# The first block of 384 tokens cut into two of 192, in a fused attention and two-layer expert kernel

## The chip, the cores and the metric

The kernel runs on one core of one Trainium2 chip. A core has TensorE (PE, matrix products; PEld is its loading of weights), VectorE (DVE), ScalarE (ACT), GpSimd (POOL) and SyncE (SP, which issues most of the transfers here). They run side by side and wait for one another by semaphores. The metric is the time of one execution on the device, in microseconds (us); lower is better.

## The reference

Inputs are float32. The batch is 8, with 8 heads, 576 positions and 64 numbers a head. Keys and values are pooled over 8 positions, so each sequence has 72 pooled positions.

```python
# attention
k_p = k.reshape(B, H, Sp, 8, D).mean(axis=3)
v_p = v.reshape(B, H, Sp, 8, D).mean(axis=3)
scores = scale * np.matmul(q, k_p.transpose(0, 1, 3, 2))
scores = scores - np.max(scores, axis=-1, keepdims=True)
attn = np.exp(scores)
attn = attn / (np.sum(attn, axis=-1, keepdims=True) + 1e-09)
x = np.matmul(attn, v_p)            # then (B*S, H*D) = (4608, 512)
# part 1: 512 -> 768 -> 512
h = np.maximum(np.maximum(x @ w1, x @ w2), x @ w3)
x = h @ w_out
# part 2: 512 -> 2048 -> 512
h = np.maximum(x @ w_in, 0.0)
out = h * h @ w_out2
```

## The kernel before

**Numbers.** A float32 operand is split into a high part and a remainder (`split`, lines 121 and 122: ScalarE copies the high part, another engine subtracts), and a product is three matmuls: high by high, high by low, low by high. The weights arrive as 64-bit numbers. Each row of 512 of them (a tile `wraw`) is loaded by SP and turned into float32 by two ScalarE and two VectorE instructions (`convert`, lines 148 to 153), and then split by ScalarE and POOL (lines 121 and 122). Part 1 has 24 such rows: 18 for w1, w2 and w3, and 6 for its output matrix.

**Part 1.** The 4608 tokens go in 12 blocks of 384. For a block, `attention(j)` fills four tiles x, one for each pair of heads, with 128 numbers by 384 tokens. For a pair it loads q (and, at the start of a sequence, k and v, which VectorE reduces over 8 positions: lines 221 and 228), splits q, multiplies q by the pooled keys in tiles of 128 or 96 tokens (line 344), takes the maximum (346), exponentials with their sums (349), adds a constant and takes the reciprocal (353, 354), scales on POOL (355), transposes (370), copies and splits the transposed scores (372, 373), and multiplies by the values (385, or 395 and 396).

A sequence has 576 tokens, so a block's tokens are one or two pieces: a piece of 384 is cut into three tiles of 128, a piece of 192 into two of 96. Block 0 is the first 384 tokens of sequence 0. Block 1 is that sequence's last 192 tokens and the first 192 of sequence 1.

In blocks with a number under `LIGHT` = 2, one softmax covers all the tiles of a pair in a piece, and POOL splits q. In the others a softmax covers one tile, and VectorE splits q.

`moe1(j)` then runs 22 steps for a block (`STEPS`). Each of the first 18 is one of three matrices by one of six groups of 128 columns: 12 matmuls (line 465), all four x, one weight row, and 384 columns. The results are copied by ScalarE (471) or joined by a maximum on VectorE (473); after three of them h is split. The last four steps multiply h by the output matrix, 18 matmuls each (484); ScalarE copies the result to ys and issues its store to y_dram. Results wait in three PSUM buffers (`mm_ps`).

**Order.** Each piece of work goes with a due time onto the list `todo`, counted in steps, and `run` writes them in the order of these times. The attention of block j+1 is spread over block j's 22 steps, shifted to the front by 10 steps; its loads stand 10 steps ahead of it and the preparation of q, k and v four. The weight rows of part 1 have due times from -12, 0.9 steps apart. The weights of part 2 are prepared in the background from block `SECOND[0]` to the last one. A scheduler then orders each engine's instructions by these priorities and by when it expects operands to be ready. Each engine works off its own list in order.

**Part 2** takes the tokens in 9 blocks of 512. It reads them back from y_dram (`load_y`, line 549 on), in as many pieces as the blocks of part 1 that they touch. Its first block is loaded and prepared during the last block of part 1.

Of the kernel before, what the change touches and what calls it, by code (L numbers as in the profile page):

```python
# [10 lines left out]
F32 = mybir.dt.float32  # L11
F32R = mybir.dt.float32r
# [8 lines left out]
P = 128  # L21
B, H, S, D = 8, 8, 576, 64
# [3 lines left out]
NT = B * S  # L26
DM = H * D
KD = DM // P
# [3 lines left out]
KF2 = FF2 // P  # L32
NE = 3
T1 = 384
NB1 = NT // T1
T2 = 512
NB2 = NT // T2

# [22 lines left out]

LEAD_SECOND = 5

SECOND = (2, NB1 - 1)

NATURAL = 1

# [17 lines left out]
def attention_moe_kernel(ctx: ExitStack, tc: tile.TileContext, q, k, v, vn, w1, w2, w3, wo1, wi2, wo2, out):  # L85
# [3 lines left out]
    dram = ctx.enter_context(tc.tile_pool(name="dram", bufs=1, space=DRAM))  # L89
    mm_ps = ctx.enter_context(tc.tile_pool(name="mm_ps", bufs=3, space=PSUM))  # L90
# [12 lines left out]

    wi2_dram = [[dram.tile([P, 2, n], F32, name=f"wi2_dram{f}_{i}") for i, n in enumerate(WIDTHS)] for f in range(KF2 // 2)]
    wo2_dram = [dram.tile([P, 2, 512], F32, name=f"wo2_dram{f}") for f in range(KF2)]
    y_dram = [dram.tile([KD, P, T1], F32, name=f"y_dram{j}") for j in range(NB1)]

# [14 lines left out]
    def split(hl, src, engine=nc.vector):  # L124

        split_to(hl[:, 0], hl[:, 1], src, engine)
# [43 lines left out]
    h_p = s1.enter_context(tc.tile_pool(name="h_p", bufs=KF1))  # L170
    t_p = s1.enter_context(tc.tile_pool(name="t_p", bufs=2))
# [87 lines left out]
    def pieces(j):  # L259

        t = 0
        while t < T1:
            b, s0 = divmod(j * T1 + t, S)
            n = min(T1 - t, S - s0)
            yield b, s0, n, t
            t += n

# [4 lines left out]
    def attention(j):  # L272

        x_t[j] = [None] * NPAIR
        n_tiles = sum(NPAIR * len(score_tiles(n)) for _, _, n, _ in pieces(j))
        pace = (STEPS - 1) / n_tiles
        at = (j - 1) * STEPS + pace / 2 - (LAG_T + LAG_V + LEAD_X)
        for b, s0, n, t in pieces(j):
            if s0 == 0 and b < NATURAL:
                tiles = []  # L280
                when = at - pace / 2 + LAG_T + LAG_V if t else at + pace / 2
                todo.append((when - LEAD_LOAD, lambda b=b, tiles=tiles: tiles.extend(load_natural(b))))
                todo.append((when, lambda tiles=tiles: pool_v(tiles)))
            for p in range(NPAIR):
                load, prepare, softmax, transpose, values = attend(j, b, s0, n, p, t)
                todo.append((at - LEAD_LOAD, load))
                todo.append((at - LEAD_PREP, prepare))
                tiles = score_tiles(n)
                if j < LIGHT:
                    todo.append((at, functools.partial(softmax, tiles)))  # L290
                for c, m in tiles:
                    if j >= LIGHT:
                        todo.append((at, functools.partial(softmax, [(c, m)])))
                    todo.append((at + LAG_T, functools.partial(transpose, c, m)))
                    at += pace
                todo.append((at - pace + LAG_T + LAG_V, values))
# [107 lines left out]
    w1_t, wo1_t = {}, {}  # L404
# [48 lines left out]
    def moe1(j):  # L453

        x = x_t.pop(j)
        hs = []
        for f in range(KF1):
            hm = t_p.tile([P, T1], F32, tag="hm", name="hm")
            h = h_p.tile([P, 2, T1], F32R, tag="h", name="h")
            for e in range(NE):  # L460
                ps = mm_ps.tile([P, T1], F32, tag="ps", name="ps")
                n = 0
                for kk in range(KD):
                    for a, c in PARTS:
                        nc.tensor.matmul(  # L465
                            ps, lhsT=w1_t[f, e][:, a, kk * P : (kk + 1) * P], rhs=x[kk][:, c],
                            start=(n == 0), stop=(n == 3 * KD - 1),
                        )
                        n += 1
                if e == 0:  # L470
                    nc.scalar.activation(hm, ps, AF.Copy)
                else:
                    nc.vector.tensor_tensor(out=hm, in0=ps, in1=hm, op=ALU.max)  # L473
                if e == NE - 1:
                    split(h, hm)
                yield
            hs.append(h)
            now[0] = hm
        for d in range(KD):
            ps = mm_ps.tile([P, T1], F32, tag="ps", name="ps")  # L480
            n = 0
            for kk in range(KF1):
                for a, c in PARTS:
                    nc.tensor.matmul(  # L484
                        ps, lhsT=wo1_t[kk][:, a, d * P : (d + 1) * P], rhs=hs[kk][:, c],
                        start=(n == 0), stop=(n == 3 * KF1 - 1),
                    )
                    n += 1
            ys = t_p.tile([P, T1], F32, tag="ys", name="ys")
            nc.scalar.activation(ys, ps, AF.Copy)  # L490
            nc.scalar.dma_start(out=y_dram[j][d], in_=ys)
            yield

    def run():
        for _, f in sorted(todo, key=lambda a: a[0]):
            f()
        todo.clear()

    def add_moe1(j):
        steps = moe1(j)  # L500
        todo.extend((j * STEPS + i, functools.partial(next, steps, None)) for i in range(STEPS))
# [6 lines left out]
    for kk in range(KF1):  # L508
        todo.append((0.9 * (NE * KF1 + kk) - 12, functools.partial(load_wo1, kk)))
    for j in range(NB1 - 1):  # L510
        add_moe1(j)
# [11 lines left out]
    for i, (src, raw, prepare) in enumerate(second):  # L523
        when = STEPS * (SECOND[0] + (i + 0.5) * (SECOND[1] - SECOND[0]) / len(second))
        todo.append((when - LEAD_SECOND, functools.partial(load_second, src, raw)))
# [23 lines left out]
    def load_y(j, r):  # L549

        yr = y_p.tile([P, 2, T2], F32, tag=f"yr{r}", name=f"yr{r}")
        for i in range(2):
            t = 0
            while t < T2:
                b, o = divmod(j * T2 + t, T1)
                n = min(T2 - t, T1 - o)
                nc.sync.dma_start(out=yr[:, i, t : t + n], in_=y_dram[b][2 * r + i, :, o : o + n])
                t += n
        yr_t[j, r] = yr
# [16 lines left out]

    ORDER = (1, 6, 7, 5, 2, 4, 3)
    early = [functools.partial(load_y, 0, r) for r in range(2)] + [functools.partial(mix_y, 0)]
    early.append(functools.partial(fetch_in, 0, w2_p))
    early += [functools.partial(split_y, 0, m) for m in ORDER]  # L580
    for i, f in enumerate(early):
        todo.append(((NB1 - 1) * STEPS + (i + 0.5) * (NE * KF1) / len(early), f))
    add_moe1(NB1 - 1)
    run()
# [85 lines left out]
    for j in range(NB2):  # L670
        for gr in range(NG):
            if gr == 0 and j + 1 < NB2:
                for r in range(2):
                    load_y(j + 1, r)
            g = moe2_in(j, gr)
            if gr == NG - 2 and j + 1 < NB2:
                mix_y(j + 1)
            if gr == NG - 1 and j + 1 < NB2:
                for m in ORDER:
                    split_y(j + 1, m)  # L680
            for h, half in ((1, 1), (0, 0), (1, 0), (0, 1)):
                moe2_out(j, gr, h, half, g[h, half])
            nxt = j * NG + gr + 1
            if nxt < NB2 * NG:
                fetch_group(*divmod(nxt, NG))
# [41 lines left out]
```

## Time and profile before

| | |
|---|---|
| median of 3 runs | 1547.24 us (1545.96 to 1547.61) |
| profiled execution | 1545.93 us, its span 1544.2 us |
| PE | 1509.4 us busy, 98% of the span, 9290 matmuls |
| DVE | 947.7 us, 61% |
| ACT | 623.0 us, 40% |
| POOL | 200.2 us, 13% |
| mean granted clock of TensorE | 0.985 |

The span runs from the first to the last instruction of the program; some 1.7 us lie around it. Busy time is the union of an engine's instructions. Matmuls are pipelined: one of 384 columns is recorded with 334 ns from start to end though the next one starts 174 ns later, so the price of a matmul is read from the distance of starts, or from the busy time of a dense run divided by its count. The granted clock is the share of TensorE's full speed that the chip allowed: 1.00 is 2.4 GHz and 0.50 is 1.2 GHz.

### The profile page before, as it was taken

Reading aid. Unit: us, or ns where it says so; the run is one execution under the profiler, and the core shown is the slowest. Engines: PE = TensorE matmul, PEld = TensorE weight load, DVE = VectorE, ACT = ScalarE, POOL = GpSimd, SP = SyncE. Lnnn points to the kernel's source line nnn. Section 1 sums busy time; section 2 is a strip of 40 time slices with the busy share of each in tenths; the row PEclk is TensorE's granted clock in tenths of the full one; section 3 lists DMA queues with packets and bytes.
Section 4 is the critical chain, followed back from the end, with each engine's and each line's share of the span. In section 5 each row is a group of like instructions: output and inputs, shape, how many; then the busy total and the mean of one; then the engine's idle time right before and its main releaser. Section 6 shows DMA issues by size and latency. Waiting matters only on the chain.

```text
span 1544.2 us, 25098 instructions
## 1 busy us (share of the span) xinstructions
PE 1509.4 (98%) x9290; PEld 1416.2 (92%) x9290; DVE 947.7 (61%) x1991; ACT 623.0 (40%) x1772; POOL 200.2 (13%) x303
## 2 busy tenths in 40 slices
PE   6899999999999999999999999999999999999998
PEld 4789999999999999999999898988989888999987
DVE  6895578776786766755427455455655546464544
ACT  7775566656566566654212212121212112121211
POOL 5550122222222121312000000000000000000000
PEclk7799999999999999999999999999999999999999
DMA  7552234434334333323475434333333433343321
GB/s 227 163 169 67 76 105 151 142 96 145 122 119 144 99 129 103 104 79 116 135 290 208 150 113 161 110 127 121 108 137 125 149 123 108 111 150 110 137 110 69
DMA packets 80858, 200.87 MB, mean 130 GB/s; under 512 B 9024, under 2 KB 32576, under 8 KB 80736
## 3 DMA queue, kind: packets, MB, share of 16 engines
q1 hardware_dynamic: 73824, 189.83, 36.2%
q10 hardware_dynamic: 6912, 9.44, 1.7%
q8 instruction: 74, 1.21, 0.3%
q14 instruction: 48, 0.39, 0.1%
HBM read 157.29 MB, written 41.94 MB: 129 GB/s over the span
## 4 chain that ended last, share of the span: by engine, by line
PE 88%; DVE 4%; DMA 3%; ACT 2%; issue 1%; SPq 0%; POOL 0%; DVEq 0%; ACTq 0%; POOLq 0%
PE ps L465 26%; PE acc L645 25%; PE ps L600 21%; PE ps L484 9%; PE sc L344 2%; PE tr L370 2%; DMA out_dram<-o 2%; PE av L396 1%; PE av L395 1%; ACT ss L349 1%; DVE wbits L153 0%; DMA kq<-in_q_dram 0%; ACT wraw L149 0%; DVE hm L473 0%; DVE wbits L150 0%
## 5 line engine op out<-in xcount | busy, mean ns | idle before, releaser
L465 PE MATMUL ps<-x,w 128*128 128x384 f32 x2592 | 508.6, 344 | 1.7 <-ACT x L121 0.8
L465 PEld LDWEIGHTS ps<-x,w 128*128 128x128 f32 x2592 | 452.0, 191 | 4.1 <-ACT x L121 1.4
L645 PE MATMUL acc<-wo2s,g 128*128 128x512 f32 x1728 | 412.6, 391 | 0.0
L600 PEld LDWEIGHTS ps<-y,wi2s 128*128 128x128 f32 x3024 | 370.4, 188 | 13.1 <-PE ps L600 4.0
L600 PE MATMUL ps<-y,wi2s 128*128 128x256 f32 x3024 | 376.8, 280 | 3.4 <-DVE s L629 2.9
L645 PEld LDWEIGHTS acc<-wo2s,g 128*128 128x128 f32 x1728 | 316.4, 188 | 62.5
L121 ACT ACTIVATE g<-c 128x512 fp32r<-128x512 f32 x144 | 90.8, 631 | 410.9 <-DVE c L611 403.9
L617 DVE TENSOR_TENSOR s<-ps,s 128x512 f32<-128x512 f32 x72 | 49.8, 691 | 262.4 <-PE ps L600 261.8
L484 PE MATMUL ps<-h,wo 128*128 128x384 f32 x864 | 164.9, 339 | 0.7 <-DVE hm L473 0.5
L484 PEld LDWEIGHTS ps<-h,wo 128*128 128x128 f32 x864 | 148.9, 188 | 1.4 <-DVE hm L473 0.8
L617 DVE TENSOR_TENSOR c<-ps,s 128x512 f32<-128x512 f32 x144 | 98.8, 686 | 24.9 <-PE ps L600 21.7
L355 POOL TENSOR_TENSOR ss<-ss,st 128x144 f32<-128x144 f32 (+3 forms) x144 | 73.2, 510 | 309.4 <-DVE st L354 237.8
L349 ACT ACTIVATE ss<-sc,st 128x72 f32<-128x72 f32 (+1 forms) x320 | 98.0, 313 | 35.0 <-DVE st L346 31.3
L473 DVE TENSOR_TENSOR hm<-ps,hm 128x384 f32<-128x384 f32 x144 | 79.4, 552 | 53.1 <-PE ps L465 49.3
L122 DVE TENSOR_TENSOR g<-c,g 128x512 fp32r<-128x512 f32 x144 | 98.6, 685 | 17.4 <-ACT g L121 16.5
L611 DVE SCALAR_TENSOR_TENSOR c<-c 128x512 f32<-128x512 f32 x144 | 98.8, 687 | 2.1
L373 DVE TENSOR_TENSOR pt<-tr,pt 72x256 fp32r<-72x256 f32 (+1 forms) x160 | 61.5, 386 | 53.4 <-ACT pt L372 52.1
L344 PEld LDWEIGHTS sc<-kbd,qs 128*128 128x128 f32 (+1 forms) x480 | 73.6, 192 | 11.4 <-issue 5.2
L344 PE MATMUL sc<-kbd,qs 128*128 128x144 f32 (+1 forms) x480 | 74.7, 271 | 8.0 <-ACT kbd L195 5.2
L372 ACT ACTIVATE pt<-tr 72x256 fp32r<-72x256 f32 (+1 forms) x160 | 56.2, 354 | 58.1 <-PE tr L370 56.5
L370 PE MATMUL tr<-ident,ss 128*72 128x128 f32 (+1 forms) x320 | 59.9, 274 | 14.4 <-DVE pt L373 10.1
L349 ACT ACTIVATION_READ_ACCUMULATOR ss<-sc,st 128x1 f32 (+1 forms) x320 | 63.1, 197 | 0.0
(78 smaller groups left out, 1249.3 us busy)
## 6 DMA issues: line engine op xcount, KB each, us to landing
wo2s<-wo_dram SPq DMA_DIRECT2D x144, 512.0 KB
wi2s<-wi_dram SPq DMA_DIRECT2D x24, 512.0 KB
wraw<-in_wo_dram SPq DMA_DIRECT2D x22, 512.0 KB
wraw<-in_w_dram SPq DMA_DIRECT2D x18, 512.0 KB
y_dram<-ys ACTq DMA_DIRECT2D x48, 192.0 KB
out_dram<-o SPq DMA_DIRECT2D x36, 256.0 KB
wraw<-in_wi_dram SPq DMA_DIRECT2D x16, 512.0 KB
wi_dram<-wraw SPq DMA_DIRECT2D x16, 512.0 KB
```

Of the source, the lines that this page charges most:

```text
L121: nc.scalar.activation(hi, src, AF.Copy)
L122: engine.tensor_tensor(out=lo, in0=src, in1=as_f32(hi), op=ALU.subtract)
L344: nc.tensor.matmul(src[:, i], lhsT=lhsT, rhs=kbd[:, p, l], start=(n == 0), stop=(n == 2))
L349: nc.scalar.activation(ss[:, i, h], src[:, i, h], AF.Exp, bias=st[:, 0, i, h : h + 1], accum_out=st[:, 1, i, h : h + 1],)
L370: nc.tensor.transpose(tr[:, h, :m], sms[c][:, h], ident[:m, :m])
L465: nc.tensor.matmul(ps, lhsT=w1_t[f, e][:, a, kk * P : (kk + 1) * P], rhs=x[kk][:, c], start=(n == 0), stop=(n == 3 * KD - 1),)
L473: nc.vector.tensor_tensor(out=hm, in0=ps, in1=hm, op=ALU.max)
L484: nc.tensor.matmul(ps, lhsT=wo1_t[kk][:, a, d * P : (d + 1) * P], rhs=hs[kk][:, c], start=(n == 0), stop=(n == 3 * KF1 - 1),)
L600: nc.tensor.matmul(bank[:, u * HT : (u + 1) * HT], lhsT=wi2_t[2 * gr + u][i][:, a, o + kk * P : o + (kk + 1) * P], rhs=y_t[j][m][:, c, kk] ...
L611: nc.vector.scalar_tensor_tensor(out=c, in0=c, scalar=0.0, in1=c, op0=ALU.max, op1=ALU.mult)
L617: nc.vector.tensor_tensor(out=c, in0=bank, in1=other, op=ALU.add)
L645: nc.tensor.matmul(acc_t[j][2 * half + i], lhsT=g[:, a, u * HT + i * P : u * HT + (i + 1) * P], rhs=wo2_t[j, 4 * gr + 2 * u + h][:, c], st ...
```

## The change

Part 1 gets a list of block sizes, `SIZES`: 192, 192, and then 384 eleven times. `NB1` becomes 13, and `BEGIN` holds the first token of each block. The tiles keep their size of 384 and the two short blocks use the first 192 columns. `STEPS` and the due times are counted in blocks as before, so each short block has 22 steps and 288 matmuls of its own. `LIGHT` remains 2, which is now the two short blocks. `SECOND` starts at block 3, which begins at the same token as block 2 did. Blocks 2 to 12 hold the tokens of the old blocks 1 to 11.

```diff
 T1 = 384
-NB1 = NT // T1
+SIZES = [T1 // 2] * 2 + [T1] * (NT // T1 - 1)
+NB1 = len(SIZES)
+BEGIN = [sum(SIZES[:j]) for j in range(NB1)]
...
-SECOND = (2, NB1 - 1)
+SECOND = (3, NB1 - 1)
...
-    y_dram = [dram.tile([KD, P, T1], F32, name=f"y_dram{j}") for j in range(NB1)]
+    y_dram = [dram.tile([KD, P, n], F32, name=f"y_dram{j}") for j, n in enumerate(SIZES)]
...
     def pieces(j):
-        while t < T1:
-            b, s0 = divmod(j * T1 + t, S)
-            n = min(T1 - t, S - s0)
+        while t < SIZES[j]:
+            b, s0 = divmod(BEGIN[j] + t, S)
+            n = min(SIZES[j] - t, S - s0)
...
     def moe1(j):
+        size = SIZES[j]
...
-            hm = t_p.tile([P, T1], F32, tag="hm", name="hm")
-            h = h_p.tile([P, 2, T1], F32R, tag="h", name="h")
+            hm = t_p.tile([P, T1], F32, tag="hm", name="hm")[:, :size]
+            h = h_p.tile([P, 2, T1], F32R, tag="h", name="h")[:, :, :size]
             for e in range(NE):
-                ps = mm_ps.tile([P, T1], F32, tag="ps", name="ps")
+                ps = mm_ps.tile([P, T1], F32, tag="ps", name="ps")[:, :size]
...
-                            ps, lhsT=w1_t[f, e][:, a, kk * P : (kk + 1) * P], rhs=x[kk][:, c],
+                            ps, lhsT=w1_t[f, e][:, a, kk * P : (kk + 1) * P], rhs=x[kk][:, c, :size],
...
-                b, o = divmod(j * T2 + t, T1)
-                n = min(T2 - t, T1 - o)
+                b = max(b for b in range(NB1) if BEGIN[b] <= j * T2 + t)
+                o = j * T2 + t - BEGIN[b]
+                n = min(T2 - t, SIZES[b] - o)
```

## Rows read from the trace of the kernel before

**Rows 1.** Busy time by stretch; the columns are named in its first line.
```profile
core 0: us, PE busy (x) PEld busy (x) DVE busy (x) ACT busy (x) POOL busy (x), PEclk, DMA share, GB/s
0.00:61.60 61.60, 41.99 (x168) 32.41 (x168) 43.34 (x89) 45.69 (x161) 35.50 (x40) 0.72 0.65 204
61.60:126.50 64.90, 60.85 (x359) 58.05 (x358) 59.54 (x129) 49.39 (x156) 29.37 (x26) 0.95 0.50 157
126.50:186.00 59.50, 59.50 (x365) 58.97 (x364) 33.20 (x90) 28.28 (x93) 6.35 (x12) 1.00 0.22 63
```

**Rows 2.** The same view, cut where the granted clock changes.
```profile
20.30:37.40 17.10, 12.19 (x47) 10.05 (x47) 14.35 (x28) 15.70 (x61) 12.43 (x12) 0.50 0.72 221
...
44.20:64.70 20.50, 18.88 (x73) 16.91 (x74) 16.88 (x37) 17.91 (x62) 10.90 (x11) 0.50 0.53 172
64.70:102.30 37.60, 34.10 (x212) 32.09 (x212) 36.56 (x69) 31.52 (x92) 21.96 (x17) 1.00 0.60 194
```

**Rows 3.** Timeline of TensorE: start us, us, engine, line, operation, shapes, count.
```profile
33.50 1.31 PE L465 MATMUL ps<-x,w 128*128 128x384 f32 x3
...
61.79 1.51 PE L385 MATMUL av<-pt,vst 72*128 72x192 f32 x6
63.10 1.99 PE L465 MATMUL ps<-x,w 128*128 128x384 f32 x6
...
76.30 0.81 PE L385 MATMUL av<-pt,vst 72*128 72x192 f32 x6
76.95 2.47 PE L465 MATMUL ps<-x,w 128*128 128x384 f32 x13
...
126.31 0.85 PE L465 MATMUL ps<-x,w 128*128 128x384 f32 x4
```

**Rows 4.** Timeline of VectorE: block 0's first and fourth x, and last h.
```profile
34.53 0.56 DVE L122 TENSOR_TENSOR x<-av,x 128x384 fp32r<-128x384 f32 x1
...
61.12 0.52 DVE L122 TENSOR_TENSOR x<-av,x 128x384 fp32r<-128x384 f32 x1
...
117.93 0.55 DVE L122 TENSOR_TENSOR h<-hm,h 128x384 fp32r<-128x384 f32 x1
```

**Rows 5.** Timeline of POOL: the last weight row of part 1.
```profile
113.87 1.28 POOL L122 TENSOR_TENSOR wo<-wbits,wo 128x512 fp32r<-128x512 f32 x1 [2.40 <-ACT wo L121]
```

**Rows 6.** Groups from 733.6 to 783.6 us: count, busy us, mean ns, idle before.
```profile
L465 PE MATMUL ps<-x,w 128*128 128x384 f32 x216 | 37.6, 334 | 0.0
L484 PE MATMUL ps<-h,wo 128*128 128x384 f32 x73 | 13.0, 334 | 0.0
```

**Rows 7.** Groups of ScalarE from 0 to 126.5 us: the exponentials and their reads.
```profile
L349 ACT ACTIVATE ss<-sc,st 128x72 f32<-128x72 f32 x38 | 11.6, 321 | 5.1 <-DVE st L346 5.0
...
L349 ACT ACTIVATION_READ_ACCUMULATOR ss<-sc,st 128x1 f32 x38 | 7.9, 208 | 0.0
```

**Rows 8.** Groups of VectorE from 0 to 61.6 us: sequence 1's reductions.
```profile
L228 DVE TENSOR_REDUCE vs<-vr 72x128 f32<-72x1024 f32 x2 | 2.4, 1216 | 3.8 <-DMA vr<-in_v_dram 3.8
L221 DVE TENSOR_REDUCE ks<-kr 128x72 f32<-128x576 f32 x3 | 2.2, 746 | 1.0 <-DMA kr<-in_k_dram 1.0
```

**Rows 9.** Groups of VectorE from 0 to 126.5 us: evacuation and light softmax.
```profile
L473 DVE TENSOR_TENSOR hm<-ps,hm 128x384 f32<-128x384 f32 x12 | 6.5, 543 | 0.0
...
L346 DVE TENSOR_REDUCE st<-sc 96x4 f32<-96x288 f32 x8 | 3.6, 446 | 1.8 <-PE sc L344 1.7
...
L353 DVE TENSOR_SCALAR st<-st 96x4 f32<-96x4 f32 x8 | 2.5, 308 | 0.9 <-ACT ss L349 0.8
L346 DVE TENSOR_REDUCE st<-sc 128x6 f32<-128x432 f32 x4 | 2.4, 600 | 2.1 <-PE sc L344 2.1
...
L399 DVE TENSOR_TENSOR xf<-av,xf 64x192 f32<-64x192 f32 x6 | 2.1, 354 | 0.7 <-ACT xf L398 0.5
...
L353 DVE TENSOR_SCALAR st<-st 128x6 f32<-128x6 f32 x4 | 1.3, 328 | 0.0
```

**Rows 10.** Groups of VectorE over the span: softmax by tile, q split.
```profile
L346 DVE TENSOR_REDUCE st<-sc 96x2 f32<-96x144 f32 x48 | 14.2, 297 | 5.3 <-PE sc L344 4.5 <-POOL wraw L132 0.4
...
L122 DVE TENSOR_TENSOR qs<-qr,qs 128x192 fp32r<-128x192 f32 x24 | 10.4, 433 | 3.0 <-ACT qs L121 2.8 <-DMA y_dram<-ys 0.2
L353 DVE TENSOR_SCALAR st<-st 96x2 f32<-96x2 f32 x48 | 10.2, 213 | 12.5 <-ACT ss L349 12.2
```

**Rows 11.** Busy time by stretch of the weight conversion alone: DVE, ACT, POOL.
```profile
61.60:126.50 64.90, 23.56 (x28) 17.09 (x27) 21.35 (x14) 0.95 0.50 157
```

More of the change, by code (lines that the diff above doesn't have):

```diff
@@ L479, in moe1 @@
         for d in range(KD):
-            ps = mm_ps.tile([P, T1], F32, tag="ps", name="ps")
+            ps = mm_ps.tile([P, T1], F32, tag="ps", name="ps")[:, :size]
             n = 0
@@ L488, in moe1 @@
                     n += 1
-            ys = t_p.tile([P, T1], F32, tag="ys", name="ys")
+            ys = t_p.tile([P, T1], F32, tag="ys", name="ys")[:, :size]
             nc.scalar.activation(ys, ps, AF.Copy)
```

## The prediction

> **What bounds the kernel now.** I read the share of each engine first: TensorE is busy 98% of the span, so a change pays or costs only what it adds to TensorE or where TensorE is not yet full. The busy time by stretch [rows 1] shows where that is: up to 61.6 us TensorE is busy 42.0 us, at a mean granted clock of 0.72; from 61.6 to 126.5 us it is busy 60.9 of 64.9 us, but VectorE is nearly as full (59.5 us); from 126.5 us on TensorE is busy all the time and VectorE has slack. The granted clock by stretch [rows 2] adds that it stood at 1.2 GHz (0.50) for 37.6 us of the first 64.7.
>
> TensorE's timeline [rows 3] puts names to these borders. Block 0's first expert matmul starts at 33.50 us and block 1's first at 126.31 us, so the two stretches are the attention of block 0 and then block 0 itself. VectorE's timeline [rows 4] shows the first x (one head pair of block 0's input) done at 35.1 us and the fourth at 61.6 us; every expert step needs all four, so block 0 cannot run dense before 61.6 us. POOL finishes the last of the 24 weight rows at 115.2 us [rows 5], and the last h follows at 118.5 us [rows 4]. So the part that the change touches is bounded by the four x until 61.6 us, then by TensorE, VectorE and the coming of the weights together. What follows 126.5 us is TensorE alone, and the change leaves it as it is: I count how much later block 2 of the new kernel (the old block 1) starts.
>
> **Matmuls: +13.3 us.** 288 matmuls of 384 columns become 576 of 192. A 384-column one costs 37.6 / 216 = 174 ns in the last block, where nothing interferes [rows 6]. The 192-column price stands in the trace too, in values matmuls with 128 weight columns: six from 76.30 to 76.95 us are 108 ns each at full clock [rows 3]. A split matmul costs 217 ns instead of 174: 288 x 43 = 12.3 us. 24 values matmuls of block 0 split likewise: 24 x 43 = 1.0 us. Scores and transposes treat the same tokens in tiles of 96 instead of 128, and I put them at nothing (ends -1 and +1 us). After 126.5 us all of this would be paid in full; before it, only the 4.0 us of TensorE's idle time [rows 1] could hide some.
>
> Here a page of the Trainium skill differs from the row. "TensorE: Matmul & The Clock Gate" (Back-to-back issue gap) gives a warm gap of N / 2.4 + 2.5 ns, 82.5 ns for 192 columns, by which the split would cost about nothing. The same page's section on loading the stationary operand (LDWEIGHTS) gives columns / 1.2, 107 ns for 128, and with the 108 ns of the row the trace agrees with this one.
>
> **A shorter prelude: -7 us.** Block 0's attention has 8 score tiles of 96 instead of 12 of 128. On ScalarE that is 16 exponentials with their reads instead of 24, at 0.53 us each [rows 7]: 4.2 us less. In the old prelude block 1 was half of sequence 1, and so three K and two V reductions of that sequence ran there (2.2 + 2.4 us on VectorE, 3.8 us of idle time before them for the V load [rows 8]); in the new one they belong to block 2, and their loads move behind those of the first weight rows on SP's queue, which lets the weights land earlier. Taken one behind the other this is 12.6 us, side by side with other work it may be nothing. ScalarE is busy 45.7 of 61.6 us and VectorE 43.3, so neither saving is fully on the path: I take 7, and the fourth x at about 54.6 us.
>
> **VectorE: +10 us, covered.** The evacuations of block 0 that take a maximum go from 12 at 0.543 us to 24 at about 0.354 (row of half width): +2.0 us [rows 9]. The first two blocks take the light path, in which one reduction serves all tiles of a pair; before they hold 768 tokens, now 384, so tokens 384 to 767 take the other path. Before: 4 x (0.600 + 0.328) + 8 x (0.446 + 0.308) = 9.7 us; after: 8 x 0.754 + 16 x (0.297 + 0.213) = 14.2 us [rows 9, 10]; +4.5 us. The light path also splits q on POOL; eight splits come to VectorE at 0.433 us: +3.5 us [rows 10]. The cover: VectorE idles 5.4 us from 61.6 to 126.5 us [rows 1], and before 126.5 us it does softmax and q splits of a block beyond, which can slip into the slack behind. Without that cover it would cost up to 5 us; that lies within the next term's end.
>
> **Weights come late for a short block: +6.7 us.** While the 14 weight rows that are left at 61.6 us are prepared (23.6 us of VectorE's 59.5 [rows 1, 11]), block 0 offers TensorE 1.30 us a step instead of 2.09, 15 x 0.79 = 11.8 us less. So it waits, and what is not done in that time is done behind. Before, the last row is ready at 115.2 us. Now it comes 7 us sooner by the prelude, and by my estimate 10 us sooner because of the 36.0 us of other VectorE work in that stretch some 10 fall behind it (the second half of the attention and half of the evacuations): at 98.2 us. Behind it stand four output steps of 18 x 108 ns (7.8 us), block 1's 288 x 108 ns (31.1 us) and some 2.4 us of attention matmuls: block 2 starts at 139.5 us. The two terms above alone would give 126.5 + 13.3 - 7 = 132.8, so this wait is 6.7 us. Its ends: 0 if the weights are always ahead, and 16.7 if they gain only the 7 us.
>
> **Other edits: nothing.** Four more stores of y and, for the first block of part 2, four more loads, lie beside the last block's 50 us of dense TensorE [rows 6]. The work on part 2's weights keeps its tokens, since its start goes from block 2 to block 3.
>
> **Sum.** 13.3 - 7 + 6.7 = 13.0 us. The profiled execution took 1545.93 us (span 1544.2 and 1.7 around it): 1558.9 us. The median of the runs is 1.3 us above it: 1560.2, so 1560 us.
>
> **Rivals.**
> - *Starved and slow.* Waiting for weights lets the granted clock fall, as from 44.2 to 64.7 us, where it was 0.50 [rows 2]. Six 192-column matmuls from 61.79 to 63.10 us then cost 218 ns each [rows 3], twice as much. With the clock down for 20 us of blocks 0 and 1 another 10 us go: +23 us, 1570 us. For it: block 0 has more waiting than before, and attention of 384 tokens now lies beside 192 tokens of matmuls. Against: from 64.7 to 102.3 us the clock held 1.00 though TensorE idled 3.5 us [rows 2].
> - *The prelude wins (faster).* TensorE's lost time lies before the fourth x. If halving the attention brings that x from 61.6 to 45 us and the weights keep up, the kernel gains 16.6 us and pays 13.3: 1544 us on the median's scale. It decides at 61.6 - 13.3 = 48.3 us: earlier than that, the split wins. For it: TensorE was idle 19.6 us there and at half clock for much of the rest. Against: it needs 16.6 us where the savings that I can list are 12.6 even end to end, and the weights' work stays in the same stretch.
> - *A 192-column matmul costs half of a 384-column one* (87 ns): then the first term is nothing, and -7 + 6.7 leaves 1547 us. Against it stand the 108 ns. This is what the gap formula of the Trainium skill's page would mean here.
> - *The added work is hidden*: TensorE's waits merely fill up, the wait for weights is 0 and the prelude gains 12 us: +1 us, 1549 us.
>
> **How the numbers follow.** My forecast has a chance of 0.68, with its own range of 1551 to 1568; starved and slow 0.14; the prelude 0.07; half price 0.06; hidden 0.05. By the bounds the sum runs from 13.3 - 12.6 = +1 to 13.3 + 16.7 = +30 us; leaving out the outer tenth on each side: 1550 to 1574. A measurement of this kernel can tell 0.2% (3.1 us) from no change. Faster: 0.07. Within: half price and half of hidden, 0.09. Slower: 0.84.
>
> **What would show it.** In the trace of the changed kernel: 192-column expert matmuls 108 to 112 ns apart in dense runs; the fourth x of block 0 at 50 to 58 us; gaps of TensorE in block 0 that end with a weight row; the last weight row near 98 us; block 2's first matmul near 139.5 us; from there to the end the same 1417.9 us. The prediction is wrong in its largest term if the 192-column matmuls come at 90 ns, and in its sign if block 2 starts before 126 us.

## The result, and the profile after

| | before | after |
|---|---|---|
| median | 1546.8 us, 4 runs (1545.96 to 1547.61) | 1570.4 us, 4 runs (1567.14 to 1571.43) |
| profiled execution, its span | 1545.93, 1544.2 us | 1570.99, 1569.2 us |
| matmuls | 9290 | 9622 |
| TensorE busy | 1509.4 us | 1538.8 us |
| mean granted clock | 0.985 | 0.975 |

The changed kernel takes 1.0149 times as long (95% interval 1.0136 to 1.0162): 23.6 us by the medians, 21 to 25 by the interval. The forecast was 1560 us, 13.0 us slower, in a range of 1550 to 1574. The four executions after were granted mean clocks of 0.975 (the profiled one), 0.976, 0.983 and 0.984 and took 1570.99, 1571.43, 1567.14 and 1569.81 us.

The borders first. TensorE's timeline of the changed kernel (start us, us; its lines 468 and 487 are the old 465 and 484):

```profile
22.18 0.74 PE L468 MATMUL ps<-x,w 128*128 128x192 f32 x2 [0.62 <-ACT w L123]
...
108.99 3.21 PE L468 MATMUL ps<-x,w 128*128 128x192 f32 x24
...
117.31 1.51 PE L468 MATMUL ps<-x,w 128*128 128x192 f32 x12
118.65 0.49 PE L387 MATMUL av<-pt,vst 72*128 72x192 f32 x3
...
149.44 1.79 PE L468 MATMUL ps<-x,w 128*128 128x384 f32 x9
```

Block 0 begins its expert matmuls at 22.18 us, block 1 at 108.99, and block 2, the old block 1, at 149.44, where it began at 126.31 before [rows 3]. That is 23.1 of the 25.0 us between the two spans. Twelve 192-column matmuls from 117.31 to 118.65 us are 112 ns apart at full clock.

VectorE's timeline of the changed kernel, with the first and the fourth x (35.1 and 61.6 us before [rows 4]):

```profile
21.08 0.36 DVE L124 TENSOR_TENSOR x<-av,x 128x192 fp32r<-128x192 f32 x1
...
44.51 0.35 DVE L124 TENSOR_TENSOR x<-av,x 128x192 fp32r<-128x192 f32 x1
```

And POOL's, with the last weight row (115.2 us before [rows 5]):

```profile
100.90 1.30 POOL L124 TENSOR_TENSOR wo<-wbits,wo 128x512 fp32r<-128x512 f32 x1 [3.03 <-ACT wo L123]
```

The fourth x comes 16.7 us earlier and the last row 13 us earlier, and yet block 2 starts 23 us later. Where that time went is seen in the busy time by stretch of the changed kernel, cut at the fourth x and at the blocks (columns as in rows 1):

```profile
0.00:44.90 44.90, 32.38 (x137) 23.91 (x137) 33.19 (x70) 35.52 (x130) 24.11 (x33) 0.70 0.64 208
44.90:109.00 64.10, 58.16 (x352) 57.11 (x352) 58.94 (x120) 43.30 (x129) 33.07 (x27) 0.69 0.52 158
109.00:149.40 40.40, 40.40 (x369) 40.40 (x369) 27.05 (x93) 23.10 (x95) 6.36 (x13) 0.99 0.28 82
149.40:209.00 59.60, 59.60 (x367) 59.05 (x366) 38.20 (x100) 30.86 (x105) 6.12 (x13) 1.00 0.23 66
```

From the fourth x to the end of block 0 the mean granted clock is 0.69; the stretch that answers to it was at 0.95 before [rows 1]. The same view of the changed kernel, cut where the granted clock changes, up to block 2:

```profile
0.00:17.60 17.60, 11.13 (x38) 5.25 (x38) 8.93 (x23) 9.40 (x35) 7.31 (x17) 1.00 0.77 257
17.60:55.10 37.50, 31.35 (x149) 28.78 (x150) 32.75 (x69) 34.35 (x123) 23.18 (x22) 0.50 0.55 174
55.10:62.00 6.90, 5.19 (x47) 4.98 (x46) 6.86 (x10) 3.88 (x8) 3.99 (x5) 0.99 0.43 149
62.00:68.80 6.80, 6.80 (x35) 6.77 (x34) 6.77 (x10) 5.79 (x15) 4.03 (x3) 0.50 0.60 199
68.80:79.00 10.20, 8.56 (x79) 8.36 (x78) 10.20 (x23) 9.39 (x32) 7.41 (x4) 1.00 0.59 189
79.00:85.80 6.80, 6.80 (x36) 6.80 (x35) 6.77 (x16) 5.22 (x19) 3.76 (x4) 0.50 0.55 166
85.80:92.70 6.90, 4.41 (x39) 4.07 (x38) 6.28 (x14) 3.65 (x8) 2.87 (x4) 0.99 0.31 83
92.70:109.70 17.00, 17.00 (x84) 16.69 (x83) 13.90 (x32) 7.60 (x29) 5.24 (x5) 0.50 0.55 151
...
sum 149.10, PE 130.63 PEld 121.11 DVE 119.18 ACT 101.66 POOL 63.54; mean PE 14.52 PEld 13.46 DVE 13.24 ACT 11.30 POOL 7.06
```

The clock stood at 0.50 for 68.1 us (37.5 + 6.8 + 6.8 + 17.0), against 41.0 before; the third half-clock stretch of before and the sum over that view (its other stretches are rows 2):

```profile
102.30:105.70 3.40, 3.40 (x14) 3.26 (x13) 3.34 (x8) 2.56 (x6) 1.41 (x2) 0.50 0.32 87
...
sum 126.50, PE 102.85 PEld 90.47 DVE 102.88 ACT 95.09 POOL 64.87; mean PE 14.69 PEld 12.92 DVE 14.70 ACT 13.58 POOL 9.27
```

From these I keep an account of TensorE (cut at 126.5 and 149.1 us, within 0.4 us of the starts of the old block 1 and the new block 2): time = idle + half of what it was busy at the clock of 0.50 (the *half-clock loss*) + the rest, its *work* in full-clock time. Up to block 1 before: idle 126.5 - 102.85 = 23.7; loss (12.19 + 18.88 + 3.40) / 2 = 17.2; work 85.6. Up to block 2 after: idle 149.1 - 130.63 = 18.5; loss (31.35 + 6.80 + 6.80 + 17.00) / 2 = 31.0; work 99.6. So the 22.6 us are +14.0 of work, -5.2 of idle time and +13.8 of half-clock loss. It is an account, not yet a cause: a slow matmul that nobody waits for costs nothing. In two stretches above (62.0 to 68.8, 79.0 to 85.8) VectorE is as full as TensorE. From 92.7 to 109.7 us TensorE is busy all 17.0 us, but the rows still come until 102.2, with VectorE busy 8.65 of the first 9.5 us. Only behind the last row is there nothing else to wait for:

```profile
102.20:109.70 7.50, 7.50 (x39) 7.50 (x39) 5.25 (x15) 4.06 (x19) 0.85 (x3) 0.50 0.75 206
```

Half of these 7.5 us, some 3.8, is what the clock surely cost in the stretch of 17.0 us in this execution; at most it is 8.5.

The runs without a trace bound it too. The half-clock loss over the span can't be more than (1 - mean clock) x span, so the execution with 0.984 lost at most 25 us, where the profiled one lost 34 and the kernel before 19. At least 9 us less of loss made it 1.2 us shorter. The one with 0.983 lost at most 27 and was 3.9 us shorter. The two average 1568.5 us, those at 0.975 and 0.976 1571.2: 2.7 us for some 8 us of loss or more. At that rate the extra loss of this change, 15 us over the span, is worth at most some 5 of the 23.6 us, an estimate from four executions.

### The profile page after: what moved, and what is told of

Read it like the earlier page. It is cut to its first block, busy times and chain, and to the rows that moved or that the text cites. A ratio compares the mean times of both kernels' runs of the same rounds, so it can differ in the third digit from the quotient of the medians.

```text
span 1569.2 us, 25931 instructions
## 1 busy us (share of the span) xinstructions
PE 1538.8 (98%) x9622; PEld 1447.7 (92%) x9622; DVE 961.5 (61%) x2061; ACT 630.4 (40%) x1816; POOL 195.9 (12%) x311
## 4 chain that ended last, share of the span: by engine, by line
PE 89%; DMA 4%; DVE 3%; ACT 2%; issue 2%; SPq 0%; POOL 0%; DVEq 0%; ACTq 0%; POOLq 0%
PE ps L468 28%; PE acc L649 24%; PE ps L604 20%; PE ps L487 9%; PE sc L346 2%; PE tr L372 2%; DMA out_dram<-o 2%; PE av L397 1%; PE av L398 1%; DVE wbits L152 1%; ACT ss L351 1%; DVE wbits L155 0%; ACT wraw L151 0%; DMA kq<-in_k_dram 0%; DMA wraw<-in_wi_dram 0%
## 5 line engine op out<-in xcount | busy, mean ns | idle before, releaser
L468 PE MATMUL ps<-x,w 128*128 128x384 f32 (+1 forms) x2808 | 527.4, 337 | 2.8 <-DVE hm L476 1.7
L468 PEld LDWEIGHTS ps<-x,w 128*128 128x128 f32 x2808 | 473.6, 196 | 4.7 <-DVE hm L476 1.9
L604 PEld LDWEIGHTS ps<-y,wi2s 128*128 128x128 f32 x3024 | 370.4, 188 | 14.8 <-PE ps L604 3.3
L487 PE MATMUL ps<-h,wo 128*128 128x384 f32 (+1 forms) x936 | 175.3, 337 | 2.4 <-DVE hm L476 2.4
L487 PEld LDWEIGHTS ps<-h,wo 128*128 128x128 f32 x936 | 159.3, 197 | 2.9 <-DVE hm L476 2.5
L357 POOL TENSOR_TENSOR ss<-ss,st 128x144 f32<-128x144 f32 (+2 forms) x156 | 77.1, 495 | 372.6 <-DVE st L356 279.6
L476 DVE TENSOR_TENSOR hm<-ps,hm 128x384 f32<-128x384 f32 (+1 forms) x156 | 81.2, 521 | 59.9 <-PE ps L468 53.3
L346 PE MATMUL sc<-kbd,qs 128*128 128x144 f32 (+1 forms) x492 | 78.7, 271 | 7.7 <-ACT kbd L197 5.3
L348 DVE TENSOR_REDUCE st<-sc 128x2 f32<-128x144 f32 (+2 forms) x156 | 47.7, 307 | 33.5 <-PE sc L346 32.0
L123 ACT ACTIVATE h<-hm 128x384 fp32r<-128x384 f32 (+1 forms) x78 | 38.9, 499 | 72.7 <-DVE hm L476 72.3
```

The costliest lines, as they stand in the source:

```text
L123: nc.scalar.activation(hi, src, AF.Copy)
L346: nc.tensor.matmul(src[:, i], lhsT=lhsT, rhs=kbd[:, p, l], start=(n == 0), stop=(n == 2))
L357: nc.gpsimd.tensor_tensor(out=ss, in0=ss, in1=st[:, 2].rearrange("p g (h o) -> p g h o", o=1).to_broadcast([m, g, 2, SP]), op=ALU.mult,)
L468: nc.tensor.matmul(ps, lhsT=w1_t[f, e][:, a, kk * P : (kk + 1) * P], rhs=x[kk][:, c, :size], start=(n == 0), stop=(n == 3 * KD - 1),)
L487: nc.tensor.matmul(ps, lhsT=wo1_t[kk][:, a, d * P : (d + 1) * P], rhs=hs[kk][:, c], start=(n == 0), stop=(n == 3 * KF1 - 1),)
L604: nc.tensor.matmul(bank[:, u * HT : (u + 1) * HT], lhsT=wi2_t[2 * gr + u][i][:, a, o + kk * P : o + (kk + 1) * P], rhs=y_t[j][m][:, c, kk] ...
```

## The experiments

All times are medians; the kernel before ran beside each, at 1546.9 to 1547.9 us.

**Accounts.** The same account over the whole span, for the profiled execution of each pair (difference to the kernel named, us):

| pair | medians | span | idle | half-clock loss | work |
|---|---|---|---|---|---|
| after - before | +23.6 | +25.0 | -4.4 | +15.2 | +14.2 |
| one VectorE instruction a row left out: after - before | +20.3 | +14.8 | -5.3 | +4.3 | +15.8 |
| both left out: after - before | +21.8 | +22.7 | -6.7 | +14.9 | +14.4 |
| no conversion: after - before | +23.6 | +23.4 | -4.6 | +13.3 | +14.7 |
| cut in the middle - before | +20.1 | +20.5 | +3.3 | +1.4 | +15.9 |
| two cuts in the middle - before | +32.8 | +34.5 | +3.0 | +3.5 | +27.9 |
| fill - after | +5.2 | +5.0 | +4.4 | -13.9 | +14.5 |

**The light path (e1).** LIGHT = 3 puts tokens 384 to 767 back on the light softmax.

```diff
-LIGHT = 2
+LIGHT = 3
```

> The changed kernel with LIGHT = 3, so that tokens 384 to 767 take the light softmax again and POOL splits their q, as before the change. Theory W (block 0 waits for weight rows that VectorE prepares, and VectorE is full from 45 to 98 us): 8 us of VectorE's work leave that stretch, some 5 of it ahead of the last weight row: 1563 to 1566 us instead of 1570. Theory L (the other softmax path is most of what was lost beyond the forecast): back to 1560 or less. Theory K (the halved clock alone, whatever VectorE does): within 2 us of 1570.

1567.8 us (ratio to before 1.0133, 1.0115 to 1.0151). The edit did what it says: a group of VectorE in its trace up to 152 us shows 16 light reductions instead of 8:

```profile
L348 DVE TENSOR_REDUCE st<-sc 96x4 f32<-96x288 f32 x16 | 7.1, 446 | 2.8 <-PE sc L346 2.8
```

It gained 2.6 us, within the intervals of both, between what theories W and K had. Theory L falls: the 8 us of VectorE that the forecast counted as covered were covered for the most part.

**The cut in the middle (e2).**

```diff
-SIZES = [T1 // 2] * 2 + [T1] * (NT // T1 - 1)
+SIZES = [T1] * 6 + [T1 // 2] * 2 + [T1] * 5
...
-SECOND = (3, NB1 - 1)
+SECOND = (2, NB1 - 1)
```

> The cut moves from the first block to the seventh (tokens 2304 to 2687, also the start of a sequence), where all weights are long there and TensorE is full. It measures the price of 192-column matmuls and of attention for 384 tokens beside 192 tokens of matmuls, without weights that come late and without a shorter prelude. Theory W and K (what exceeds the matmuls' price is the start's doing): 288 x 46 ns + 1 us = 14 us over the kernel before, 1560 to 1562. Rival C (crowded attention beside a short block costs by itself): 20 us or more over it, 1567 and above.

1568.1 us (ratio 1.0135, 1.0118 to 1.0152): 20.1 us, so rival C. The stretches of its trace from the block ahead of the cut to the block behind it:

```profile
367.00:422.50 55.50, 55.50 (x345) 55.11 (x344) 29.76 (x74) 26.57 (x80) 8.14 (x17) 1.00 0.28 96
422.50:508.90 86.40, 82.26 (x743) 80.80 (x742) 72.20 (x223) 60.95 (x240) 28.94 (x50) 1.00 0.46 152
```

And the same tokens in the kernel before:

```profile
367.00:488.10 121.10, 120.93 (x758) 119.01 (x757) 88.01 (x237) 75.12 (x254) 30.90 (x53) 1.00 0.37 121
```

141.9 us against 121.1, all at full clock. Of the 20.8 us 4.0 are new idle time of TensorE in the two short blocks, where VectorE is now busy 72.2 of 86.4 us; the other 16.8 are matmul time. So the cut costs nearly the same here, without an earlier x, without late rows and without a lower clock, as it does at the start (23.6 us).

**Two cuts (e9)** tells the price of a cut from what is paid once.

```diff
-SIZES = [T1 // 2] * 2 + [T1] * (NT // T1 - 1)
+SIZES = [T1] * 6 + [T1 // 2] * 4 + [T1] * 4
...
-SECOND = (3, NB1 - 1)
+SECOND = (2, NB1 - 1)
```

> Four blocks of 192 in the middle, in place of the seventh and the eighth block of 384; with one of them cut (two blocks of 192) it was 20 us over the kernel before. Theory P (price of the split alone, 20 us a block): 40 us, 1587. Rival C (15 us of matmuls a block, and 4 to 5 us once, where attention for 384 tokens stands beside 192 tokens of matmuls): 33 to 36 us, 1580 to 1583.

1579.7 us (ratio 1.0213, 1.0199 to 1.0227): 32.8 us. The second cut costs 12.7 us, near the forecast's 13.3, and some 7 us are paid once: just under rival C's 33 to 36, and theory P, with its 40, falls. The account agrees, with 27.9 us of work for two cuts.

**Cheaper weight rows, three doses (e3, e7, e8).** First one VectorE instruction of each row's conversion is left out, in both kernels:

```diff
-        nc.vector.scalar_tensor_tensor(
-            out=a, in0=high, scalar=-0x80000000, in1=a, op0=ALU.bitwise_and, op1=ALU.bitwise_or
-        )
+        if after is not None:
+            nc.vector.scalar_tensor_tensor(
+                out=a, in0=high, scalar=-0x80000000, in1=a, op0=ALU.bitwise_and, op1=ALU.bitwise_or
+            )
```

> The changed kernel with one of the two VectorE instructions left out in the conversion of each of part 1's 24 weight rows (the sign is not put in, so all part 1 weights are positive): some 20 us of VectorE's work less before block 2. Theory W: the weights come earlier by 12 to 18 us, and the kernel falls from 1570 to 1554 to 1560. Theory K (clock without weights): it falls by 4 us or less. To be read beside the same edit of the kernel before.

> The kernel before with the same VectorE instruction left out of part 1's 24 weight rows. Theory W: a block of 384 tokens has matmuls to cover the weights with, so this one gains less than the changed kernel does: 4 to 8 us, 1539 to 1543, and the distance between the two shrinks from 23.6 to about 16 us (the matmuls' price and little else). Rival: both gain the same and the distance stays at 20 us or more, which would say that VectorE's weight work is not what the change ran into.

1557.0 us after (ratio to the kernel before 1.0063, 1.0044 to 1.0081) and 1536.7 before (0.9926, 0.9907 to 0.9945). Both gain about alike, 13.4 and 11.3 us, and they stay 20.3 us apart. That is theory W's miss: the changed kernel was to gain far more. The profiled executions lie only 14.8 us apart, and in them the half-clock loss differs by 4.3 us alone. But of four executions each the trace has the fastest after (1554.8 to 1559.9 us) and the slowest before (1534.9 to 1540.0), so that this row of the table shows the distance too small.

Then both VectorE instructions go, by the same condition around the pair:

> The changed kernel with both VectorE instructions of the conversion left out of part 1's 24 weight rows (their bits are not put together), 40 us of VectorE's work less before block 2; a stronger dose than the one instruction, whose pair left the medians 20 us apart. Theory W/V: without VectorE's bound only TensorE's work is left over, and the earlier fourth x counts: 1540 to 1548, 8 to 15 us over the same edit of the kernel before. Theory P (the split costs 20 us wherever and whatever): 20 us over it.

> The kernel before with both VectorE instructions left out of the conversion of part 1's 24 weight rows. Theories W/V: 1530 to 1535. The distance to the changed kernel with the same edit decides: 8 to 15 us by W/V, 20 us by theory P.

1558.3 us (1.0075, 1.0062 to 1.0088) and 1536.5 (0.9933, 0.9919 to 0.9947): nothing more is gained, and the distance is 21.8 us, not the 8 to 15 of theories W and V. The stretch from the fourth x to the last row says why. The changed kernel with this edit, then the one before with it (third engine column VectorE, fourth ScalarE):

```profile
43.80:82.20 38.40, 35.41 (x265) 34.86 (x265) 20.89 (x62) 36.33 (x113) 24.67 (x25) 0.83 0.58 188
```

```profile
58.10:99.70 41.60, 39.57 (x243) 38.00 (x242) 27.93 (x63) 36.41 (x114) 21.63 (x21) 0.96 0.60 193
```

VectorE has slack, and ScalarE is busy 36.3 of 38.4 us: the bound went to the other engine that prepares the rows. So the third dose takes out the conversion of both:

```diff
-        split(w, convert(raw_pool, load_raw(raw_pool, src)), nc.gpsimd)
+        split(w, as_f32(load_raw(raw_pool, src)[:, :, 1]), nc.gpsimd)
```

> The changed kernel with the conversion of part 1's 24 weight rows left out altogether: no VectorE and only one of three ScalarE instructions a row; the split takes the raw high words, so part 1's weights are other numbers. Without VectorE's share ScalarE had no slack either while the rows came (idle 2.1 of 38.4 us in the changed kernel, 5.2 of 41.6 in the one before), so the earlier pairs only passed the bound on. Theory W' (the engines that prepare the rows, VectorE and ScalarE together, hold both kernels, and a block of 192 offers TensorE half the work meanwhile): now the earlier fourth x counts, and it stands 5 to 15 us over the same edit of the kernel before. Theory P (20 us is the price of the split anywhere): 20 us over it.

> The kernel before with the conversion of part 1's 24 weight rows left out altogether. Both theories: faster than with VectorE's part left out alone (1536.5 us), 1524 to 1533. The distance to the changed kernel decides: 5 to 15 us by W', 20 us by P.

1551.7 us (1.0035, 1.0021 to 1.0049) and 1528.1 (0.9882, 0.9866 to 0.9899). Each is 19 us faster than without the edit, and they are 23.6 us apart, exactly as the kernels themselves. W' falls too: how dear the rows are moves both kernels, and not their distance. (Theory P's 20 us fit these pairs; that they are not the price of the split alone is shown by the two cuts.) POOL's timeline of the changed kernel with this edit has its last row, and the stretches by clock behind it show what block 0 then waits for:

```profile
64.45 1.30 POOL L124 TENSOR_TENSOR wo<-wraw,wo 128x512 fp32r<-128x512 f32 x1 [1.48 <-ACT wo L123]
```

```profile
18.30:49.10 30.80, 27.02 (x136) 26.02 (x137) 21.50 (x45) 22.25 (x93) 25.40 (x26) 0.50 0.81 271
49.10:59.30 10.20, 8.46 (x76) 8.28 (x76) 3.75 (x10) 5.33 (x15) 7.87 (x8) 1.00 0.86 287
59.30:72.90 13.60, 13.60 (x68) 13.60 (x68) 7.12 (x16) 4.01 (x12) 3.33 (x3) 0.50 0.57 156
72.90:130.90 58.00, 58.00 (x536) 58.00 (x536) 39.81 (x136) 33.03 (x144) 8.87 (x18) 1.00 0.29 82
```

From 59.3 to 72.9 us the clock is at 0.50 while TensorE is busy all the time, VectorE 7.1 us, ScalarE 4.0 and POOL 3.3 of 13.6: nothing but the clock holds it, and half of that stretch is lost. The rows that come until 65.8 us belong to the output matrix, and TensorE is still at the expert steps. The kernel before with the same edit has its full clock from 44.6 us to its block 1:

```profile
44.60:111.30 66.70, 63.02 (x402) 60.30 (x401) 46.37 (x109) 41.75 (x151) 25.58 (x27) 1.00 0.52 166
```

**Filling TensorE (e4).**

```diff
             for e in range(NE):
                 ps = mm_ps.tile([P, T1], F32, tag="ps", name="ps")[:, :size]
+                if j == 0:
+                    for i in range(6):
+                        nc.tensor.matmul(
+                            ps, lhsT=w1_t[f, e][:, i % 2, :P], rhs=x[0][:, i // 3, :size],
+                            start=(i == 0), stop=(i == 5),
+                        )
```

> The changed kernel, with six more matmuls of 192 columns ahead of each of block 0's first 18 steps, whose sums are overwritten: 108 matmuls, 12 us of TensorE at full clock, put where it waits. Theory K (the halved clock is what the start loses: 31 us against 17 before): the clock stays up for some 20 us more, and the kernel falls to 1560 or less. Theory V (VectorE bounds the start, and a halved clock only fills what would be idle time): the clock rises, idle time takes its place, and the kernel stays at 1568 to 1578.

1575.6 us (1.0188, 1.0174 to 1.0203), as V has it and not K. The clock did rise. The stretches of its trace in block 0, up to its end at 110.1 us, and on to block 2:

```profile
59.70:87.00 27.30, 22.82 (x191) 21.42 (x189) 26.71 (x35) 19.15 (x37) 16.34 (x13) 1.00 0.55 179
87.00:93.80 6.80, 6.22 (x29) 6.23 (x30) 6.74 (x14) 2.58 (x7) 1.40 (x2) 0.50 0.44 134
93.80:110.10 16.30, 16.30 (x153) 16.30 (x153) 10.65 (x34) 8.20 (x36) 2.56 (x4) 1.00 0.37 113
110.10:152.30 42.20, 42.20 (x392) 42.20 (x391) 30.55 (x107) 26.89 (x113) 6.72 (x15) 1.00 0.27 77
```

Block 0 ends at 110.1 us instead of 109.0 though it holds 108 more matmuls, 12 us at 110 ns: 13.9 us of half-clock loss are gone, and the fill's own work took their place. While the clock is full, VectorE is busy 26.71 of 27.30 us, so there it is the bound. A clock that is bought with as much work as it gives back gains nothing.

**Both halves beside one another (e5).**

```diff
-        todo.extend((j * STEPS + i, functools.partial(next, steps, None)) for i in range(STEPS))
+        todo.extend(({0: 1.5 * i, 1: 17 + 1.2 * i}.get(j, j * STEPS + i), functools.partial(next, steps, None)) for i in range(STEPS))
...
-                x_t[j][p] = x_p.tile([P, 2, T1], F32R, tag="x", name="x")
+                if j != 1:
+                    whole_x[p] = x_p.tile([P, 2, T1], F32R, tag="x", name="x")
+                x_t[j][p] = whole_x[p][:, :, T1 // 2 :] if j == 1 else whole_x[p]
```

(h is shared between the halves in the same way, and block 0's hm has a buffer of its own.)

> The changed kernel with the steps of block 1 mixed among those of block 0 (due times 17 + 1.2 i and 1.5 i; both halves share the tiles x and h), so that each weight row has 384 tokens of matmuls soon after it comes. Theory W (a block of 192 gives TensorE too little to do while the rows come, and the second half is done behind the last row): the second half's work moves ahead of the last row, 5 to 12 us, 1558 to 1565. Theory V alone (VectorE's total work up to block 2, however TensorE's is placed): within 3 us of 1570.

1570.8 us (1.0155, 1.0141 to 1.0170): V's number. But the trace shows that the test missed its point. VectorE's timeline has the second half's last x, and the busy time by clock:

```profile
87.78 0.34 DVE L124 TENSOR_TENSOR x<-av,x 128x192 fp32r<-128x192 f32 x1
```

```profile
18.70:90.40 71.70, 61.09 (x288) 57.28 (x287) 67.88 (x115) 59.63 (x174) 41.27 (x36) 0.50 0.55 178
```

The second half's x is not there before 88.1 us, so its matmuls could not go beside the rows, and block 0's own steps, due later, left the clock at 0.50 for 71.7 us on end. It says nothing on W.

**Rows first (e6).**

```diff
-            todo.append((0.9 * (NE * f + e) - 12, functools.partial(load_w1, f, e)))
+            todo.append((0.5 * (NE * f + e) - 12, functools.partial(load_w1, f, e)))
...
-        todo.append((0.9 * (NE * KF1 + kk) - 12, functools.partial(load_wo1, kk)))
+        todo.append((0.5 * (NE * KF1 + kk) - 12, functools.partial(load_wo1, kk)))
```

> The changed kernel with part 1's weight rows due 0.5 steps apart instead of 0.9, so that they go ahead of the second block's attention on VectorE and ScalarE. Theory W': the last row comes 5 to 12 us sooner than 102 us, but block 1's attention later by as much; what is behind the last row grows: 1566 to 1572. A rival (the order alone is what holds block 0): 1560 or less.

1570.2 us (1.0150, 1.0133 to 1.0168). POOL's timeline has the last row at 97.1 us, 5.1 sooner, and block 2 starts at 148.0 instead of 149.4; the order of the rows is not what holds the changed kernel.

```profile
95.54 1.55 POOL L124 TENSOR_TENSOR wo<-wbits,wo 128x512 fp32r<-128x512 f32 x1 [2.23 <-ACT wo L123]
```

No variant that keeps the cut came near the same kernel without it.

## Why the prediction was right, and where its sum was off

The direction and the range held; of the 23.6 us the sum named 13.0.

**Matmuls, +13.3.** Right. The dense runs are 112 ns apart, the account has 14.2 us of added work, and the second cut in the middle cost 12.7 us. The 192-column price taken from six values matmuls of the kernel before held to 4 ns. The half-price rival (87 ns) falls. With the Trainium skill's "TensorE: Matmul & The Clock Gate" the trace agrees in the section on LDWEIGHTS (columns / 1.2, an estimate of 107 ns for 128). The 82.5 ns of its section on the back-to-back gap are no contradiction: that section calls its formula the gap of an isolated matmul and says that it comes out too low at small N where each matmul has its own weight load, which the 112 ns bear out.

**A shorter prelude, -7.** The mechanism was right, its size was not what counted. The fourth x came at 44.9 us, 9.7 us sooner than forecast. But 17 of the 24 rows were then still to come, where it had been 14 before (their conversion takes 30.4 us of VectorE's time, against 23.6 [rows 11]), and the stretch from the fourth x to the last row became longer, with VectorE nearly full in both (the changed kernel, then the one before):

```profile
44.90:102.20 57.30, 51.36 (x318) 50.31 (x319) 54.00 (x106) 39.71 (x112) 32.82 (x26) 0.71 0.50 153
```

```profile
61.60:115.20 53.60, 49.55 (x288) 46.82 (x287) 52.22 (x105) 41.83 (x126) 27.06 (x22) 0.94 0.52 166
```

TensorE's idle time over the span fell by 4.4 us only.

**VectorE, covered.** It held as far as it was tested: the light path back on POOL gains 2.6 us, not told from nothing.

**Weights come late, +6.7.** This is the term that was mis-sized. By the prediction's own sum (132.8 us without it) it measures 16.6 us, since block 2 started at 149.4 us and not at 139.5; that is the upper end which the prediction gave it. Of the 9.9 us between, 4.0 are the last row, forecast at 98.2 us and there at 102.2. The rest lies behind that row. The output steps were near (6.8 us against 7.8), but block 1 took 40.4 us instead of 33.5: at 112 ns its 288 matmuls make 32.3, which leaves, as an estimate, 8 us for the other matmuls, the attention of block 2, of which the forecast had put 2.4 there.

Its cause failed too. The three doses show that the distance of the two kernels does not hang on the rows: it is 23.6 us as they are, and 20.3, 21.8 and 23.6 us with ever cheaper ones. The half-clock loss does not fill the gap either, though it is the largest new entry of the account (+15.2 us): from +1.4 with the cut in the middle to +15.2 at the start, the distance goes from 20.1 to 23.6 us alone (idle time moves the other way, from +3.3 to -4.4), and by the changed kernel's own executions it is worth at most some 5 us. It is on the path for some 3.8 us behind the last row of the changed kernel and for 6.8 us in the third dose. The rest lies beside a nearly full VectorE, where the fill shows that a faster clock turns into idle time.

What stands is this: some 13 to 14 us of work for each cut, and beyond it some 9 us at the start and some 7 in the middle. By the times, the earlier x at the start has paid for none of it.

**The rival "starved and slow"** had 1570 us, the measured time, at a chance of 0.14. That it met the time is luck in good part. The clock did stay down, for 27 us longer up to block 2, but by the estimate above that was worth at most some 5 us and not the rival's 10. And it is not missing rows that keep it down: in the third dose all rows are there at 65.8 us and it stays at 0.50 until 72.9, under a TensorE without a gap. The stretch that the rival named for it, 44.2 to 64.7 us before, has TensorE busy 18.9 of 20.5 us, and so does not show that waiting lowers the clock.

**The prelude rival** had half of its condition met (the fourth x at 44.9 us, before 48.3) and not the other half: the weights did not keep up, and the kernel was slower.

**Left open.** Why the clock stays at 0.50 longer is not shown, only that it does in each of the four pairs of kernels with the cut at the start (by 3 to 31 us over the span); 192-column matmuls in the middle ran at 1.00. A fill that holds the clock and costs no work was not tried. What the 7 to 9 us beyond the work are is traced in part only: in the middle 4.0 are idle time with a crowded VectorE. A rival for the rest was not run: due times are counted in steps, so that the attention of a block of 384 is spread over the 22 steps of a block half as long. The same due times counted in tokens would test it.

## What to carry to other kernels

Cutting a block halves the columns of a matmul but not its time: where 384 columns cost 174 ns, 192 cost some 110, so a cut of 288 matmuls costs 13 to 14 us of TensorE wherever it is, and a quicker start has to earn that first. What an earlier start earns is the work that can run at once: count the stretch behind it with the engines that feed it, and count what the next block's attention needs behind the last row. An account of idle time, half-clock loss and work, the same for each variant, shows in one table which term an edit moves, but not what the term is worth: that took pairs of kernels, and executions of one kernel with different clocks.

## What the runs showed of the hardware

The clock stayed at 0.50 for 17.0 us through which TensorE was, by the profile, busy without a gap (92.7 to 109.7 us after), and for 13.6 us in the third dose, and rose only then to 1.00, where it stayed under dense 192-column matmuls (39.4 and 58.0 us). Before, it rose at 64.7 us after 20.5 us in which TensorE was busy 18.9. A mean granted clock of 0.984 in place of 0.975 made the same kernel only 1.2 us faster. Taking VectorE's 40 us from the preparation of the rows gained no more than taking 20, and ScalarE was then busy 36.3 of 38.4 us; with two of its three instructions a row gone as well the kernel gained 6.6 us more.
